# Block 4's scores alternate between two heads, a weight conversion runs two tiles ahead, and raw weights load in four pieces

## The chip, the cores and the metric

The kernel runs on one core of a Trainium2 chip. The metric is the device time of one execution in microseconds (us). Engines are named as in the profile: PE is TensorE's matmul, PEld its weight load, DVE is VectorE, ACT ScalarE, POOL GpSimd, SP SyncE. In this kernel every DMA is issued from SP, whose queue is in order: an issue that waits holds back all that stand behind it.

## The reference

Three layers follow each other. Attention works on q, k, v of shape (4, 8, 576, 64): causal softmax scores per head, with a second term from a stored memory `M_prev`, mixed by a gate.

```python
scores = scale * q @ k.T; masked above the diagonal; a = softmax(scores); local = a @ v
q_p = phi(q); mem_out = (q_p @ M_prev) / (q_p @ z_prev + 1e-6)
out = g * mem_out + (1 - g) * local
```

Its output, as x of 2304 tokens by 512, goes into MoE 1, a gated layer with d_ff = 1536: `x = (silu(x @ w_gate) * (x @ w_val)) @ w_out`. MoE 2 has 8 experts of width 1024 and a balanced router:

```python
P = exp(x @ w_gate - max)
for _ in range(8):                       # Sinkhorn
    P /= P.sum(1) + 1e-9; P /= P.sum(0) + 1e-9; P *= N / E
out = sum(P[:, e] * (relu(x @ w1[e]) @ w2[e]) for e in range(8))
```

## The kernel before

Matmuls are made from pairs of rounded parts: a value is split into a high part and the rest, and a product is three matmuls (high by high, high by low, low by high). `product` (L461) issues them for one output; `products` (L283) issues each of the three for all outputs of a list before the next one.

The source is not the order of the engines. The framework traces the program, and a list scheduler then orders each engine's instructions at compile time, by source order and by when its own cost model holds an instruction ready. An instruction that is ready by that model can so be put ahead of others written before it; on the chip each engine then runs its list in order. `issue_after(i)` binds each instruction of a block that is on the engine of `i` to stand behind `i`.

**Attention** (L147) handles 16 pairs of heads. Each has generators for its stages: `load`, `prepare`, `scores`, `normalize`, `transposed`, `values`. A written schedule, `BEGIN`, `ORDER` for the middle pairs and `END`, advances them one step at a time, several pairs interleaved; `S` is a step of `scores`. One pair's two heads lie on partitions 0 to 63 and 64 to 127, so a score matmul contracts over 64 rows. Query blocks are taken in the order 4, 3, 2, 1, 0. Blocks 3 to 1 (L344) compute both heads into one PSUM tile through `products`, which alternates the heads. Block 4 (L329) takes head 0 and then head 1, each a `ps` tile of its own, 576 keys as two halves of 288 columns; each head has 6 matmuls, one mask matmul (L336), a maximum on DVE (L338), an exponential on ACT (L339) and a `yield`. The pool `pss` has two buffers of two banks each. Block 0 (L364) is the last of a pair; its exponentials are L371.

**MoE 1** (L594) begins behind attention. Its weights arrive as 64-bit floats and are converted on the chip, 12 slices of the hidden width with 3 tiles each, 36 tiles. `load_unit` (L491) does a tile: a DMA of the raw words (`graw`, 3 buffers), then `narrow` (L469): ACT takes the magnitude (L481), POOL clips it (L482), DVE shifts (L483), restores the sign (L484), ACT rounds the high part (L485), DVE forms the low bits (L486 to L488); then a subtraction on DVE (L505) and a DMA that keeps the parts in DRAM for later passes (L506). `self.ahead` is the generator over all tiles. Two tiles are done at the end of attention, bound behind its last exponential, and `on()` (L610) advances `ahead` by one tile, or, when that is used up, the first generator of `aside`. The first pass computes token chunks 0 and 1 together, slice by slice, with `on(4)` ahead of it and three `on()` in each slice; the two matmul groups `hidden` end in a Silu on ACT (L618) and a product on DVE (L619). Later passes read the kept parts. Their `aside` work is, for a chunk that is done, the router's `logits` (L532: four copies and subtractions into `xl`, 2 buffers, eight matmuls, four transposes, in one step) and `parts` (L563: seven tiles of sums of x, split and written to DRAM by L561).

**MoE 2** (L976) takes 16 units of weights (half an expert each), and for each unit four chunks of 512 tokens (p = 0 to 3) and one of 256. `order` (L1021) is a string of steps: H is one group of 12 matmuls of `unit_hidden` (L884) on a tile `xr` of x, O one output group (`unit_out`, L956). `right` (L1002) loads `xr` through 5 buffers up to five tiles ahead. `prepare_unit` (L800) loads the next unit's raw weights as one DMA of 2 MB (L805; one buffer), then sums and splits them on POOL, ACT and DVE, one `yield` between the steps; it is advanced once a step from the first chunk's seventh step on. During unit 0 `aside` does the remaining logits and parts and the Sinkhorn iteration, at every second step of p = 0 and every step later.

## Time and profile before

| | |
|---|---|
| Time, median of three runs | 2288.07 us (2285.83 to 2288.82) |
| Profiled execution, time | 2287.38 us |
| Its span, first to last instruction | 2285.6 us |
| PE busy | 97% |
| DVE, ACT, POOL busy | 52%, 32%, 20% |
| Mean granted TensorE clock | 0.995 |

The span is what the instructions cover; the time has 1.8 us more around it. In the profile attention covers about the first 254 us, MoE 1 up to about 732 us, and MoE 2 the rest. Busy shares are means over stages with different limits: DVE is busy for 134.2 of the 152 us from 255 to 407 us and for about 45 of 96 us in a unit of MoE 2. A PE that is called busy can run at either clock.

### The profile page before, as it was taken

What the parts mean: (1) busy time and instruction counts of PE and PEld (TensorE: products, weight loads), DVE (VectorE), ACT (ScalarE), POOL (GpSimd) and SP (SyncE); (2) the same over time, 40 slices, a digit from 0 to 9 for tenths busy, and PEclk for the clock granted to TensorE, in tenths of its full rate; (3) what the DMA queues carried; (4) which work ended last, traced back from release to release, by engine and by line L of the source; (5) the groups of instructions that cost most, each with busy time, mean ns of one, the idle gap of its engine ahead of it and who ended that gap; (6) DMA issues with size and microseconds to landing.
All of it is one profiled execution on the core that took longest, in us unless ns stands there. A gap on an engine that the chain in (4) does not pass through costs nothing.

```text
span 2285.6 us, 33742 instructions
## 1 busy us (share of the span) xinstructions
PE 2224.9 (97%) x13490; PEld 1909.6 (84%) x13490; DVE 1191.8 (52%) x1915; ACT 737.1 (32%) x1452; POOL 466.2 (20%) x425
## 2 busy tenths in 40 slices
PE   8999898999999999999999999999999999999999
PEld 5666676778888788898888988888888898888998
DVE  7888788541413744544455444544445444454433
ACT  6887533331312322222222222222222222222221
POOL 6666555210201121101011010110101101011000
PEclk9999899999999999999999999999999999999999
DMA  4221477365532746546465464654646556465563
GB/s 167 102 102 66 139 236 233 123 233 212 190 135 100 283 132 223 196 145 227 143 230 194 147 221 147 227 192 154 221 145 221 192 162 212 142 227 195 164 200 133
DMA packets 112188, 406.45 MB, mean 178 GB/s; under 512 B 11680, under 2 KB 11680, under 8 KB 108960
## 3 DMA queue, kind: packets, MB, share of 16 engines
q1 hardware_dynamic: 112032, 404.29, 52.1%
q8 instruction: 108, 1.77, 0.3%
q14 instruction: 48, 0.39, 0.1%
HBM read 364.92 MB, written 39.32 MB: 177 GB/s over the span
## 4 chain that ended last, share of the span: by engine, by line
PE 82%; DMA 7%; DVE 5%; POOL 3%; issue 1%; ACT 1%; SPq 0%; ACTq 0%; DVEq 0%; POOLq 0%
PE po L465 37%; PE pt L884 13%; PE pc L884 10%; PE p L465 8%; DMA xr<-xp 6%; PE pt L947 4%; PE po L437 2%; PE pt L404 2%; POOL na L482 2%; PE ps L465 1%; PE ps L287 1%; POOL w L821 1%; DMA graw<-gvo 1%; PE pp L465 1%; ACT w L819 1%
## 5 line engine op out<-in xcount | busy, mean ns | idle before, releaser
L465 PE MATMUL po<-w,h 128*128 128x512 f32 x3456 | 835.2, 392 | 3.9 <-DVE nm L773 3.9
L465 PEld LDWEIGHTS po<-w,h 128*128 128x128 f32 x3456 | 631.5, 188 | 125.4 <-DVE nm L773 4.0
L884 PE MATMUL pt<-xr,w 128*128 128x256 f32 x3072 | 403.9, 280 | 0.0
L884 PEld LDWEIGHTS pt<-xr,w 128*128 128x128 f32 x3072 | 381.8, 188 | 6.8
L972 DVE SCALAR_TENSOR_TENSOR xacc<-po,Pw,xacc 128x512 f32<-128x512 f32 x270 | 202.3, 749 | 287.0 <-PE po L465 287.0
L465 PE MATMUL p<-xs,gw 128*128 128x512 f32 (+1 forms) x1440 | 312.8, 373 | 14.5 <-DVE hf L619 5.7
L884 PEld LDWEIGHTS pc<-xr,w 128*128 128x128 f32 x2304 | 296.5, 188 | 33.9 <-ACT w L819 19.3
L884 PE MATMUL pc<-xr,w 128*128 128x256 f32 x2304 | 305.8, 280 | 14.0 <-DMA xr<-xp 14.0
L465 PEld LDWEIGHTS p<-xs,gw 128*128 128x128 f32 x1440 | 253.3, 190 | 65.6 <-DVE hf L619 7.8
L891 ACT COPY m<-pc 128x512 f32<-128x512 f32 x192 | 112.2, 584 | 523.8 <-PE pc L884 523.8
L896 DVE TENSOR_TENSOR m<-pt,m 128x512 f32<-128x512 f32 x256 | 176.3, 690 | 191.2 <-PE pt L884 131.5
L903 ACT ACTIVATE h<-m 128x512 fp32r<-128x512 f32 x256 | 162.0, 633 | 285.9 <-DVE m L896 280.5
L904 DVE SCALAR_TENSOR_TENSOR h<-m,h 128x512 fp32r<-128x512 f32 x256 | 178.0, 696 | 79.1 <-ACT h L903 75.1
L815 POOL TENSOR_TENSOR w<-raw,w 128x512 fp32r<-128x512 f32 x17 | 22.5, 1322 | 745.9 <-ACT w L814 745.9
L465 PE MATMUL po<-h,ws 128*128 128x512 f32 x576 | 137.4, 390 | 0.0
L465 PEld LDWEIGHTS po<-h,ws 128*128 128x128 f32 x576 | 108.3, 188 | 22.8
L821 POOL TENSOR_TENSOR w<-raw,w 128x512 fp32r<-128x512 f32 x32 | 56.1, 1753 | 340.1 <-ACT w L819 340.1
L815 DVE TENSOR_TENSOR w<-ws,w 128x512 fp32r<-128x512 f32 x64 | 79.6, 1262 | 46.3 <-ACT w L814 44.2
L318 POOL TENSOR_SCALAR P<-P,sums 128x576 f32<-128x576 f32 (+4 forms) x160 | 94.6, 605 | 42.6 <-ACT ph L263 32.3
L482 POOL TENSOR_SCALAR na<-na 128x512 f32<-128x512 f32 x36 | 84.6, 2353 | 72.7 <-ACT na L481 56.9
L947 PEld LDWEIGHTS pt<-xr,w 128*128 128x128 f32 x768 | 94.3, 188 | 2.7
L619 DVE TENSOR_TENSOR sg<-sg,p 128x512 f32<-128x512 f32 (+1 forms) x48 | 29.6, 617 | 126.5 <-PE p L465 102.7
(180 smaller groups left out, 1989.4 us busy)
## 6 DMA issues: line engine op xcount, KB each, us to landing
xr<-xp SPq DMA_DIRECT2D x480, 512.0 KB, 4.1
raw<-w SPq DMA_DIRECT2D x16, 2048.0 KB, 8.1
gw<-kg SPq DMA_DIRECT2D x24, 1024.0 KB, 4.8
graw<-gvo SPq DMA_DIRECT2D x36, 512.0 KB, 4.2
xp<-xl SPq DMA_DIRECT2D x30, 512.0 KB, 3.3
kg<-gw SPq DMA_DIRECT2D x24, 512.0 KB, 3.8
ws<-ko SPq DMA_DIRECT2D x24, 512.0 KB, 4.7
qk<-qkv SPq DMA_DIRECT2D x16, 640.0 KB, 4.0
```

Source lines behind the costliest of these rows:

```text
L318: nc.gpsimd.tensor_scalar(t, t, r, 1.0, op0=ALU.mult, op1=ALU.mult)
L465: self.nc.tensor.matmul(out, lhs[a], rhs[b], start=start and n == 0, stop=stop and n == 2, skip_group_check=shared)
L482: nc.gpsimd.tensor_scalar(a, a, pattern(0x40000000), pattern(0x4FEFFE00), op0=ALU.max, op1=ALU.min)
L815: lo.tensor_sub(t[:, 1], q[name], f32(t[:, 0]))
L821: engine.tensor_sub(t[:, 1, j], raw[:, 2 * n + j, 1], f32(t[:, 0, j]))
L884: nc.tensor.matmul(out[:, j * HT:(j + 1) * HT], w[:, a, j, k], x[:, b, k], start=start and j + k + n == 0, stop=k + n == 3, skip_group_che ...
L891: nc.scalar.copy(t, src)
L896: nc.vector.tensor_add(c, *terms)
L903: nc.scalar.activation(t[:, 0], c, AF.Relu)
L904: nc.vector.scalar_tensor_tensor(t[:, 1], c, 0.0, f32(t[:, 0]), op0=ALU.max, op1=ALU.subtract)
L947: nc.tensor.matmul(ph[:, j * HT:(j + 1) * HT], w[:, b, j, k], x[:, c, k], start=j + a + k + i == 0, stop=a + k + i == 4, skip_group_check= ...
L972: nc.vector.scalar_tensor_tensor(acc, po, weight, acc, op0=ALU.mult, op1=ALU.add)
```

## The change

Attention: block 4 takes both `ps` tiles at once and issues its 12 matmuls with the heads alternating, then both masks; the maxima and exponentials follow one head a step, as before. MoE 1: the first two of a tile's operations after its DMA (magnitude on ACT, clip on POOL) move into `load_raw`, which is called two tiles ahead of the rest. The first three tiles' `load_raw` is called when the steps of `END` begin, outside the binding to the last exponential. Tiles are taken in an order that puts a slice's third tile one slice later. `on(4)` becomes `on(2)`, and `graw`, `na`, `nb` get 4, 4 and 3 buffers in place of 3, 3 and 4. `logits` yields after each split and before the transposes. MoE 2: the raw weights load as four DMAs of 512 KB, a step apart, and in the main loop these loads, like the DMAs of `aside`, are bound behind the latest `xr` load in SP's order; in unit 0 `aside` is advanced at every step.

```diff
@@ attention
-            for step, at in schedule(n):
+            steps = schedule(n)
+            for nth, (step, at) in enumerate(steps):
+                if nth == len(steps) - len(END.split()) and after:
+                    self.ahead = self.load_units()
+                    next(self.ahead)
@@ scores
-        for j, h in enumerate(HALVES):
-            ps = self.pss.tile([P, 2, 512], F32, name="ps")
-            for c in range(2):
-                self.product(
-                    ps[:, c, 0:hw], cut(q, h, slice(4 * P, 5 * P)), cut(k, h, slice(c * hw, (c + 1) * hw)), True, c != j
-                )
-            d = slice(0, P) if j == 0 else slice(hw - P, hw)
-            nc.tensor.matmul(ps[:, j, d], self.mask, self.identb, start=False, stop=True)
+        both = [self.pss.tile([P, 2, 512], F32, name="ps") for _ in HALVES]
+        for c in range(2):
+            for a, b in ((0, 0), (0, 1), (1, 0)):
+                for j, h in enumerate(HALVES):
+                    nc.tensor.matmul(
+                        both[j][:, c, 0:hw], q[a][h, 4 * P:5 * P], k[b][h, c * hw:(c + 1) * hw],
+                        start=a + b == 0, stop=a == 1 and c != j,
+                    )
+        for j, d in enumerate((slice(0, P), slice(hw - P, hw))):
+            nc.tensor.matmul(both[j][:, j, d], self.mask, self.identb, start=False, stop=True)
+        for j in range(2):
+            ps = both[j]
@@ narrow: magnitude and clip go to load_raw
-        nc.scalar.activation(a, high.bitcast(F32), AF.Abs, scale=65536.0)
-        nc.gpsimd.tensor_scalar(a, a, pattern(0x40000000), pattern(0x4FEFFE00), op0=ALU.max, op1=ALU.min)
@@ load_unit becomes load_raw and load_units
+    def load_raw(self, f, a):
+        raw = self.rawp.tile([P, 512, 2], I32, name="graw")
+        nc.sync.dma_start(raw, self.gvo[f, :, a].bitcast(I32).rearrange("p (n t) -> p n t", t=2))
+        t = self.nap.tile([P, 512], F32, name="na")
+        nc.scalar.activation(t, raw[:, :, 1].bitcast(F32), AF.Abs, scale=65536.0)
+        nc.gpsimd.tensor_scalar(t, t, pattern(0x40000000), pattern(0x4FEFFE00), op0=ALU.max, op1=ALU.min)
+        return raw, t
+    def load_units(self):
+        todo = sorted(((f, a) for f in range(NF1) for a in range(3)), key=lambda t: (t[0] + (t[1] == 2), t[1]))
+        begun = [self.load_raw(*t) for t in todo[:3]]
+        yield
+        for n, (f, a) in enumerate(todo):
+            if 0 < n < len(todo) - 2:
+                begun.append(self.load_raw(*todo[n + 2]))
...
+            w = self.narrow(*begun[n], parts[:, 0])
             nc.vector.tensor_sub(parts[:, 1], w, f32(parts[:, 0]))
             nc.sync.dma_start(kept, f32(parts))
             yield
@@ logits
             nc.vector.tensor_sub(t[:, 1], src, f32(t[:, 0]))
+            yield
...
         nc.vector.tensor_copy(lt[:, 0:m * P], pl[0:2 * E, 0:m * P])
+        yield
@@ moe1
-            on(4)
+            on(2)
@@ prepare_unit
-        nc.sync.dma_start(raw, self.w12[e, f:f + 4].rearrange("f p a n -> p f a n"))
-        yield
+        for n in range(4):
+            nc.sync.dma_start(raw[:, n], self.w12[e, f + n])
+            yield
@@ moe2
-                        nc.sync.dma_start(f32(tiles[-1]), self.xparts[q][k])
+                        self.last_load = nc.sync.dma_start(f32(tiles[-1]), self.xparts[q][k])
+            def behind(steps):
+                with tc.issue_after(self.last_load.ins):
+                    return next(steps, None)
-                        if u == 0 and (p or at % 2):
-                            next(aside, None)
+                        if u == 0:
+                            behind(aside)
-                            late = next(prep, None) == "late" or late
+                            late = behind(prep) == "late" or late
@@ body
-                for n, b in (("graw", 3), ("na", 3), ("nb", 4))
+                for n, b in (("graw", 4), ("na", 4), ("nb", 3))
```

## Rows read from the trace of the kernel before

**Rows 1.** The page, part 1: busy us, share of the span, instructions.
```profile
PE 2224.9 (97%) x13490; PEld 1909.6 (84%) x13490; DVE 1191.8 (52%) x1915; ACT 737.1 (32%) x1452; POOL 466.2 (20%) x425
```
**Rows 2.** PE's waits over the whole span: us in total, times, longest.
```profile
PE pc L884 <- DMA xr<-xp: 14.0, 15, 2.1
...
PE pt L404 <- DVE xacc L378: 5.9, 1, 5.9
PE p L465 <- DVE hf L619: 5.7, 5, 2.1
PE p L465 <- DVE sg L619: 4.8, 3, 2.1
PE p L542 <- DVE xl L540: 4.7, 5, 2.0
PE po L465 <- DVE nm L773: 3.9, 1, 3.9
PE p L465 <- DVE xs L457: 1.9, 1, 1.9
...
PE ps L287 <- ACT P L339: 1.6, 1, 1.6
...
PE po L542 <- DVE xl L540: 0.9, 1, 0.9
```
**Rows 3.** Three stretches: length, busy us (instructions) by engine, PEclk, DMA share, GB/s.
```profile
243.90:250.72 6.82, 5.63 (x23) 3.74 (x24) 4.84 (x12) 2.86 (x6) 0.95 (x1) 0.50 0.29 93
264.38:271.20 6.82, 5.80 (x14) 4.55 (x15) 5.01 (x10) 2.95 (x5) 4.60 (x2) 0.50 0.61 230
397.50:400.91 3.41, 3.41 (x10) 2.64 (x9) 3.22 (x7) 1.17 (x2) 2.03 (x1) 0.50 0.39 154
```
**Rows 4.** PE in order of time, one middle pair: start us, us, instruction.
```profile
107.38 0.40 PE L465 MATMUL ps<-KH,QH 64*128 64x288 f32 x1
...
108.37 0.23 PE L336 MATMUL ps<-identb,mask 128*128 128x128 bf16 x1
...
108.97 0.40 PE L465 MATMUL ps<-KH,QH 64*128 64x288 f32 x1
...
109.96 0.23 PE L336 MATMUL ps<-identb,mask 128*128 128x128 bf16 x1
...
111.50 0.47 PE L287 MATMUL ps<-KH,QH 64*128 64x448 f32 x2
...
112.31 0.29 PE L353 MATMUL ps<-identb,mask 128*128 128x128 bf16 x2
```
**Rows 5.** ACT in order of time, the same pair.
```profile
107.25 0.31 ACT L371 ACTIVATE P<-ps,nm 64x64 f32<-64x64 f32 x1
```
**Rows 6.** DVE in order of time, end of attention: idle before it and its releaser last.
```profile
241.06 1.48 DVE L483 TENSOR_SCALAR na<-na 128x512 int32<-128x512 int32 x1 [1.06 <-POOL na L482]
242.46 2.35 DVE L484 SCALAR_TENSOR_TENSOR na<-graw,na 128x512 int32<-128x512 int32 x2
244.73 0.21 DVE L378 COPY xacc<-pt 128x64 f32<-128x64 f32 x1
```
**Rows 7.** MoE 1's first pass, the stretch (columns as rows 3).
```profile
255.00:407.00 152.00, 138.29 (x578) 110.34 (x577) 134.22 (x236) 58.01 (x97) 79.83 (x34) 0.97 0.67 220
```
**Rows 8.** DVE by line, the same stretch: busy us, mean ns, idle before and releaser.
```profile
L483 DVE TENSOR_SCALAR na<-na 128x512 int32<-128x512 int32 x34 | 16.5, 489 | 14.6 <-POOL na L482 14.6
```
**Rows 9.** SP in order of time, unit 2 to 3 of MoE 2.
```profile
950.45 0.38 SPq L805 DMA_DIRECT2D raw<-w  x1
```
**Rows 10.** Landing of the five xr loads issued from 950.9 to 956.1 us.
```profile
DMA to landing us min/median/max: 9.8/9.9/10.4
```
**Rows 11.** The page, part 6: DMA issues, KB each, median us to landing.
```profile
xr<-xp SPq DMA_DIRECT2D x480, 512.0 KB, 4.1
raw<-w SPq DMA_DIRECT2D x16, 2048.0 KB, 8.1
```
**Rows 12.** ACT's waits from 239 to 407 us.
```profile
ACT na L481 <- DMA graw<-gvo: 49.2, 22, 4.0
```

More of the change, by code (lines that the diff above doesn't have):

```diff
@@ L467, in product, with narrow @@
             )
-    def narrow(self, raw, hi):
+    def narrow(self, raw, a, hi):
         nc = self.nc
-        n = raw.shape[1]
         low, high = raw[:, :, 0], raw[:, :, 1]
-        a = self.nap.tile([P, n], F32, name="na")
-        b = self.nbp.tile([P, n], F32, name="nb")
+        b = self.nbp.tile([P, 512], F32, name="nb")
         ai, bi = a.bitcast(I32), b.bitcast(I32)
-        nc.scalar.activation(a, high.bitcast(F32), AF.Abs, scale=65536.0)
-        nc.gpsimd.tensor_scalar(a, a, pattern(0x40000000), pattern(0x4FEFFE00), op0=ALU.max, op1=ALU.min)
         nc.vector.tensor_scalar(ai, ai, 4, 1, op0=ALU.logical_shift_left, op1=ALU.logical_shift_right)
@@ L489, in narrow @@
         return b
-    def load_unit(self, f):
+    def load_raw(self, f, a):
         nc = self.nc
-        for a in range(3):
-            raw = self.rawp.tile([P, 512, 2], I32, name="graw")
-            nc.sync.dma_start(raw, self.gvo[f, :, a].bitcast(I32).rearrange("p (n t) -> p n t", t=2))
+        raw = self.rawp.tile([P, 512, 2], I32, name="graw")
[5 more added lines that the diff above has]
+    def load_units(self):
+        nc = self.nc
+        todo = sorted(((f, a) for f in range(NF1) for a in range(3)), key=lambda t: (t[0] + (t[1] == 2), t[1]))
[4 more added lines that the diff above has]
+                begun.append(self.load_raw(*todo[n + 2]))
             if a == 0:
-                self.gw[f] = t = self.gwp.tile([P, 2, 2, 512], F32R, name="gw")
+                self.gw[f] = self.gwp.tile([P, 2, 2, 512], F32R, name="gw")
             if a < 2:
-                parts, kept = t[:, :, a], self.keptg[f][:, :, a]
+                parts, kept = self.gw[f][:, :, a], self.keptg[f][:, :, a]
             else:
-                self.ws[f] = t = self.wsp.tile([P, 2, 512], F32R, name="ws")
-                parts, kept = t, self.kepto[f]
-            w = self.narrow(raw, parts[:, 0])
+                self.ws[f] = self.wsp.tile([P, 2, 512], F32R, name="ws")
+                parts, kept = self.ws[f], self.kepto[f]
+            w = self.narrow(*begun[n], parts[:, 0])
             nc.vector.tensor_sub(parts[:, 1], w, f32(parts[:, 0]))
@@ L529, in open_early @@
         self.gw, self.ws = {}, {}
-        self.ahead = (step for f in range(NF1) for step in self.load_unit(f))
     def logits(self, psum, name, pool, first, last):
@@ L658, in more @@
                 if logits:
-                    self.logits(pgv, "p0", self.xl, t0 // P, (t0 + n) // P)
-                    yield
+                    yield from self.logits(pgv, "p0", self.xl, t0 // P, (t0 + n) // P)
                 yield from self.parts(c)
@@ L804, in prepare_unit @@
         e, f = u // 2, u % 2 * 4
-        nc.sync.dma_start(raw, self.w12[e, f:f + 4].rearrange("f p a n -> p f a n"))
-        yield
+        for n in range(4):
+            nc.sync.dma_start(raw[:, n], self.w12[e, f + n])
+            yield
         w1, w2 = self.w1[u], self.w2[u]
@@ L988, in start_up @@
                 for c in range(2, len(CHUNKS1)):
-                    self.logits(self.po, "po", xl, *(sum(CHUNKS1[c][0:k]) // P for k in (1, 2)))
-                    yield
+                    yield from self.logits(self.po, "po", xl, *(sum(CHUNKS1[c][0:k]) // P for k in (1, 2)))
                 yield from self.parts(PAIRS2 - 1)
```

## The prediction

> **What bounds the kernel now.** I read the page's busy shares first: PE works 2224.9 of 2285.6 us [rows 1], so no other engine bounds the whole, and a change pays only where PE waits, where it runs at the lower clock, or where its own work shrinks. Then the waits on PE [rows 2]: they are short and lie in four places, the end of attention (5.9), MoE 1's first pass (DVE's products L619, 5.7 and 4.8, and 1.9 for `xs`), the router's logits (4.7), and MoE 2 (3.9 once in unit 0, and 14.0 in 15 waits for `xr`). Third, the granted clock: three stretches behind such waits stand at 0.50, the 1.2 GHz level of the two (1.2 and 2.4 GHz) [rows 3]. Fourth, PE in order of time within a middle pair of attention, because the first part changes its own work [rows 4]. Last, who made DVE late: in MoE 1's first pass DVE is busy for 134.2 of 152 us [rows 7], and 14.6 of the rest it stands before L483 until POOL's clip is done [rows 8]. DVE is full there, and what it does in the wrong order PE pays for.
>
> **1. Block 4's scores.** One head's six matmuls of 288 columns run from 107.38 to its mask at 108.37, the other's from 108.97 to 109.96: 0.99 us each [rows 4]. Blocks 3 to 1, already alternating, show what two heads cost: six matmuls of 448 columns, both heads, take 0.81 us from 111.50 to the mask at 112.31, in rows of two that start together; 64 rows of one head and 64 of the other run side by side. Six pairs should so take what six singles take now, and one 0.99 goes per pair: 16 x 0.99 = 15.8. Against it: the second head now needs the second `ps` buffer at once and not 1.6 us later. That buffer holds the pair before's block 0, whose last exponential ends at 107.25 + 0.31 = 107.56 [rows 5], 0.18 after PE would start. With the way from ACT to PE I take 0.25 for 15 pairs: 3.8. That leaves 12.0. The top is 15.8; at the bottom each pair waits as long as PE's one wait for an exponential of this kind, 1.6 [rows 2], and 15.8 - 16 x 1.6 = -9.8. I take the value by the steady pair's own times, since that 1.6 is at the start. The Trainium skill, TensorEngine Tiling (Array Packing), section PSUM Bottleneck, says that packing speeds up the matmuls but not the emptying of PSUM; the 0.18 is that in this trace, and by the rule at its worst the gain would be the bottom just given.
>
> **2. End of attention.** The 5.9 us wait of L404 is for a DVE copy at 244.73 that empties a PSUM buffer. DVE is in order; before the copy stand L483 and L484 of the first two tiles, L483 waiting for POOL's clip (1.06 before the second) [rows 6]. The clips come late because magnitude and clip are bound behind the last exponential. In the change the first three are free of that bind, and their work is hidden where PE is the bound. DVE's operations may still stand ahead of the copy, 1.48 + 2.35 us for the last three of them, but can begin when DVE falls idle. Behind the wait PE did 5.63 us of work at half clock [rows 3], worth 2.8. So 8.7 at most; if 3.8 us of DVE work stays ahead, 5.9 - 3.8 = 2.1 and no clock, at least. I take 6.5, nearer the top.
>
> **3. Start of MoE 1.** `on(2)` puts four conversions, not six, ahead of the split of the second chunk; two conversions are up to 2 x 134.2 / 34 = 7.9 us of DVE (the 134.2 include products and splits [rows 7, 8]), more than the wait of 1.9 for `xs`. The half clock at 264.4 costs 5.80 / 2 = 2.9 [rows 3]. Together 4.8; I take 4.0, and 0 below. The missing fifth and sixth tiles aren't felt: slice 1 needs only tiles 0 to 3.
>
> **4. The rest of the first pass.** Waits for L619 of 10.5 (5.7 + 4.8), and 3.41 / 2 = 1.7 of clock: 12.2. With clips two tiles ahead DVE loses up to 14.6 of waiting, needs 137 for what took 152, and PE, busy 138.3 [rows 7], becomes the bound, barely. I take 9.0, because the two are so close that some products will still be late; 0 if POOL stays the slow one, 12.2 at the top. The added buffer of `graw` lets the DMA start one tile earlier and is what feeds this.
>
> **5. Logits in MoE 1.** The 4.7 us [rows 2] are PE standing between a split and its matmuls; now a step of matmul work lies between. I take 4.0, bounds 0 and 4.7. The twelve steps and the end of the generator make 13 `on()`, of which slice 0 has 13; the second chunk's leave one tile of `parts` behind the pass, some 1 us of ACT and DVE beside PE, cost 0 to 0.7.
>
> **6. Start of MoE 2.** The 0.9 for logits goes. The 3.9 stays: Sinkhorn's first copy L773 stands in DVE behind splits that wait for buffers of `xl`, and the writes that free these now queue in SP behind `xr` loads that wait for PE. I take 1.0; from -3.0 (the wait doubles, 0.9 - 3.9) to 4.8.
>
> **7. Raw weights.** The 2 MB load is issued at 950.45 [rows 9]. It takes 8.1 us to land, a load of 512 KB 4.1 [rows 11], and the five `xr` loads behind it take 9.8 to 10.4 [rows 10]: one queue, served in order. In the change a piece goes in behind the latest `xr` load, so the load that PE misses (issued at 950.93, held behind the 2 MB) passes ahead of all four; the next have one or two pieces before them, 2 us each (a quarter of 8.1), and are needed one to three steps later. I take 12.5 of the 14.0, bounds 0 and 14.0. Next late would be the unit's first sums on POOL, which wait for the last piece some 2 us longer, with the rest of the unit to catch up. Three more DMA issues a unit cost SP 3 x 0.38 [rows 9], beside PE.
>
> **Sum.** 12.0 + 6.5 + 4.0 + 9.0 + 4.0 + 1.0 + 12.5 = 49.0. The profiled execution took 2287.4 (span 2285.6 and 1.8 around it), 0.7 below the median: 2287.4 - 49.0 + 0.7 = 2239. All tops together, 15.8 + 8.7 + 4.8 + 12.2 + 4.7 + 4.8 + 14.0 = 65.0, give 2223.
>
> **Rivals.**
> - *MoE 1 stays bound by DVE* (parts 2 to 4 come out at a third, 6.5 for 19.5): 2239 + 13 = 2252. For it: DVE's 134.2 and PE's 138.3 are 4 us apart, and POOL's clips still run beside DVE. Against: the 14.6 us are waits, not work. 16%.
> - *PSUM eats the first part* (bottom of 1): 2239 + 21.8 = 2261. For it: two buffers, both taken at once. Against: the 0.18 above. 8%.
> - *Slower: ACT takes the magnitude of tile n+2 ahead of the rounding of tile n.* It stands so in the source; ACT then waits for the raw DMA with the rounding behind it, and DVE's last subtraction behind that. ACT's present wait for these DMAs is 49.2 us over 22, 2.2 each [rows 12]; 33 times 2.2 on DVE's path is 73, where the stretch has 152 - 134.2 = 18 spare: +55, and parts 2 to 4 gone: 2239 + 19.5 + 55 = 2313. It decides from a wait of (49.0 - 19.5 + 18) / 33 = 1.4 us a tile. For it: these waits exist. Against: ACT's list goes by readiness, and a fourth buffer gives the DMA a tile more of time. 6%.
> - *Slower: each piece pays a landing of its own*: 4 x 4.1 - 8.1 = 8.3 us later per unit, and the 15 units' waits grow by as much, +124: 2376. Against: the five `xr` loads behind the 2 MB were issued over 5.2 us and all landed within 10.4 [rows 10], so they don't add up. 2%. The Trainium skill, DMA: Bandwidth & Descriptors, section Bandwidth, asks for DMAs of at least 1 MiB, which speaks against the pieces; rows 10 speak against paying for it here.
> - *The lists come out as before*, since the scheduler decides: within 5 us of 2288. 3%.
>
> **How the numbers follow.** The forecast has 65%, with a range of its own of 2226 to 2252. The first two rivals (24%) are faster too. Slower is 8%, no change 3%, faster 89%; the run-to-run spread lets 0.2%, 4.6 us, be told from no change. The range is 2221 to 2268: it holds the forecast and the two near rivals, and leaves out the last three and some of their surroundings.
>
> **What would show it.** Part 1: block 4's matmuls as rows of two, a pair's period some 0.75 us shorter from one block 4 to the next, no wait for L371 over 0.3. Parts 2 to 4: no wait of L404 over 2.5 us, DVE's wait at L483 under 5 us in total, no stretch at 0.50 before 400 us. Part 5: waits at L542 under 1 us. Part 7: `xr` waits under 2 us in total, a unit some 0.9 us shorter. The forecast fails if DVE's first pass doesn't shorten, or if any new wait of PE exceeds 10 us in total.

## The result, and the profile after

The changed kernel takes 2267.13 us (2266.72 to 2267.34) beside 2288.45 for the kernel before: a ratio of 0.9909 [0.9889, 0.9928], faster by 21.3 us where 49 were forecast. The median is over four executions; one of them took 2649.98 us at a granted clock of 0.772, and the range and the ratio leave it out. The profiled execution took 2266.92 us, its span is 2264.8 and its granted clock 0.995, as before.

Three marks divide a span: the first matmul of block 4 in each of the 16 pairs, the first matmul of MoE 1 (`p<-xs,gw`) and the first of MoE 2 (`pc<-xr,w`). They are read from PE in order of time, and the same marks serve for every experiment below.

| us | before | after | difference | forecast |
|---|---|---|---|---|
| first matmul of MoE 1 (attention) | 254.2 | 264.3 | +10.1 | -18.5 (parts 1, 2) |
| from there to MoE 2 | 477.9 | 458.8 | -19.1 | -17.0 (parts 3 to 5) |
| from there to the end | 1553.6 | 1541.7 | -11.9 | -13.5 (parts 6, 7) |
| span | 2285.6 | 2264.8 | -20.8 | -49.0 |

So MoE 1 and MoE 2 gave about what was forecast, and the whole miss lies in attention, which became longer. Within it, block 4 of the sixth pair starts at 86.1 us (79.1 before), and from there the period of a pair is 14.86 (14.15 before). That is +7.0 in the first five pairs and +0.7 in each of the ten after them; the end of attention gives 3.8 back.

The busy shares of the page, part 1:

```profile
PE 2219.6 (98%) x13490; PEld 1904.9 (84%) x13490; DVE 1205.4 (53%) x1915; ACT 735.0 (32%) x1452; POOL 466.7 (21%) x425
```

PE's busy time fell by 5.3 us of 2224.9 [rows 1], for the same 13490 instructions. The rest of the gain is waiting. Waits on PE over the whole span (us in total, times, longest), which answer to [rows 2]:

```profile
...
PE pt L413 <- POOL P L322: 5.1, 12, 1.7
PE pt L904 <- DMA xr<-xp: 4.9, 1, 4.9
PE po L474 <- DVE xacc L988: 4.2, 1, 4.2
PE ps L291 <- ACT P L348: 4.1, 2, 3.5
PE pt L413 <- DVE xacc L387: 3.7, 1, 3.7
PE p L474 <- DVE sg L639: 3.6, 2, 2.8
PE ps L291 <- ACT P L368: 1.8, 10, 0.3
...
PE po L561 <- DVE xl L558: 1.0, 1, 1.0
PE p L474 <- DVE hf L639: 0.9, 1, 0.9
...
PE ps L338 <- ACT P L380: 0.3, 1, 0.3
```

The 15 waits of 14.0 for `xr` are gone, and so are those for `xl` in MoE 1 (the 1.0 that is left is in MoE 2); the products `sg` and `hf` keep PE 4.5 us where it was 10.5. New are the waits for POOL's P (L322), one of 4.9 for `xr` and one of 4.2 for `xacc`, both in unit 0. The wait for block 4's exponentials (L348, before L339) grew from 1.6 to 4.1, of which 3.5 stand in the first pair. The wait for the second `ps` buffer, L338 behind the exponential L380, is 0.3 once.

**A middle pair.** PE in order of time, the changed kernel (start, us, instruction):

```profile
115.76 0.40 PE L338 MATMUL ps<-KH,QH 64*128 64x288 f32 x1
...
116.11 0.40 PE L338 MATMUL ps<-KH,QH 64*128 64x288 f32 x1
...
117.10 0.28 PE L343 MATMUL ps<-identb,mask 128*128 128x128 bf16 x2
117.22 0.61 PE L403 MATMUL pt<-ident,ph 128*128 128x128 f32 x4
...
119.15 1.07 PE L446 MATMUL po<-T,vm 128*64 128x512 f32 x2
120.15 0.47 PE L291 MATMUL ps<-KH,QH 64*128 64x448 f32 x2
...
121.17 1.07 PE L446 MATMUL po<-T,vm 128*64 128x512 f32 x2
122.18 0.55 PE L413 MATMUL pt<-ident,P 128*128 128x128 f32 x3
```

The same view of the kernel before, places of the pair that [rows 4] did not reach:

```profile
108.44 0.60 PE L394 MATMUL pt<-ident,ph 128*128 128x128 f32 x4
...
110.12 0.87 PE L437 MATMUL po<-T,vm 128*64 128x384 f32 x4
...
112.53 1.08 PE L437 MATMUL po<-T,vm 128*64 128x512 f32 x4
113.53 0.66 PE L404 MATMUL pt<-ident,P 128*128 128x128 f32 x4
```

Block 4 with its masks takes 117.22 - 115.76 = 1.46 us. Before it was 1.06 for head 0 (107.38 [rows 4] to 108.44) and 1.15 for head 1 (108.97 to 110.12), so 0.75 is saved, as forecast. The price of the second buffer is in it: head 1's first matmul comes at 116.11, 0.35 after head 0's and 0.14 after ACT is done with the buffer (its last exponential of block 0, L380, runs from 115.66 to 115.97). Until then head 0's run alone, and head 1's last ones do so at the end. As PE is not idle meanwhile, no wait of that size shows. But the value products of 512 columns, which the change doesn't touch, come out otherwise. Before, four stand in a row, two of each head, and take 1.00 us from start to next start. After, head 0's two stand at 119.15 and head 1's two at 121.17, with block 3's scores between them, and each two take the 1.00 that four took. Each of these matmuls fills 64 of 128 columns (`128*64`): two heads' ran side by side where they were neighbours in the list, and not where block 3's scores stood between them. The Trainium skill, TensorEngine Tiling (Array Packing), section Key Properties, says that different tiles "can execute LdWeights and Matmul in parallel"; these rows agree, with 1.00 against 2.01, and add that the order of the list decides whether they do.

One whole pair as a stretch (length, busy us by engine, PEclk, DMA share, GB/s), first after, then before:

```profile
115.76:130.62 14.86, 14.50 (x99) 8.86 (x98) 13.97 (x27) 11.55 (x35) 9.29 (x15) 1.00 0.31 97
```
```profile
107.38:121.53 14.15, 14.15 (x100) 9.18 (x99) 11.71 (x27) 11.58 (x35) 9.79 (x14) 1.00 0.29 102
```

PE's work: 14.15 - 0.75 + 1.00 = 14.40, where the row has 14.50. The other 0.36 are two waits of 0.17 and 0.19 in this pair, L291 behind ACT's exponential L368 and L413 behind POOL's P. Together 14.86.

**The first pairs.** The first three tiles' magnitude and clip have only a DMA to wait for, so they stand at the start of attention and not at its end. What DVE does on these tiles stands there too. The bind behind the last exponential holds back what ACT does (the rounding, L489), but not DVE's shift, sign and low bits (L487, L488, L490 to L492), which need only the clip: fifteen operations, some 10 us, between 33.69 and 69.05 us. Clips and operations together are the early conversions below. POOL in order of time, the changed kernel:

```profile
31.74 5.68 POOL L503 TENSOR_SCALAR na<-na 128x512 f32<-128x512 f32 x3
37.91 2.42 POOL L322 TENSOR_SCALAR P<-P,sums 128x576 f32<-128x576 f32 x3 [0.49 <-DVE sums L299]
```

DVE and then PE in the same stretch:

```profile
35.58 0.82 DVE L487 TENSOR_SCALAR na<-na 128x512 int32<-128x512 int32 x1 [1.06 <-POOL na L503]
...
37.66 0.15 DVE L299 TENSOR_TENSOR sums<-sums,gs 128x4 f32<-128x4 f32 x1
```
```profile
38.81 0.66 PE L413 MATMUL pt<-ident,P 128*128 128x128 f32 x4 [1.71 <-POOL P L322]
```

Three clips hold POOL for 5.68 us. DVE, in order, stands 1.06 before a shift until the second clip is done, and the sums of the pair (L297 to L299) come between and behind its operations on the tiles. The P of the pair needs POOL and these sums: it waits 0.49 more for the sums when the clips are done, and PE waits 1.71 for P. Without these tiles (e3 below) the same P starts at 35.12 and not at 37.91. Two stretches, first after, then before:

```profile
25.20:40.80 15.60, 12.90 (x86) 7.31 (x85) 11.62 (x24) 13.02 (x39) 14.22 (x16) 1.00 0.25 88
40.80:56.60 15.80, 13.21 (x88) 8.46 (x86) 14.34 (x30) 9.18 (x26) 10.68 (x13) 0.89 0.45 130
47.60:51.02 3.42, 3.42 (x17) 2.08 (x17) 3.23 (x8) 2.29 (x8) 1.24 (x2) 0.50 0.79 245
```
```profile
24.00:36.00 12.00, 11.98 (x81) 7.65 (x80) 9.08 (x19) 10.88 (x37) 9.78 (x14) 1.00 0.26 90
36.00:50.70 14.70, 14.70 (x93) 9.02 (x92) 10.51 (x26) 10.76 (x30) 8.70 (x15) 1.00 0.29 99
```

Before, PE was full in the second and third pair. After, it is busy 12.90 of 15.60 and 13.21 of 15.80 us, and there is a stretch at half clock (47.60 to 51.02). In the third pair DVE is busy for 14.34 of 15.80 us, where it was 10.51 of 14.70.

**The end of attention.** DVE in order of time, the changed kernel, which answers to [rows 6]:

```profile
253.93 1.48 DVE L487 TENSOR_SCALAR na<-na 128x512 int32<-128x512 int32 x1 [2.73 <-POOL na L503]
...
256.05 0.22 DVE L387 COPY xacc<-pt 128x64 f32<-128x64 f32 x1
```

This is the fourth tile. Its magnitude is called two tiles ahead, and so still within the bind behind the last exponential; its shift stands in DVE ahead of the copy that PE waits 3.7 for, and waits 2.73 for its clip, as the first two tiles' did before.

**MoE 1's first pass.** The stretch that answers to [rows 7], and DVE's shift in it that answers to [rows 8]:

```profile
264.30:416.30 152.00, 146.29 (x633) 119.04 (x632) 132.25 (x226) 58.33 (x100) 79.39 (x33) 0.99 0.66 219
```
```profile
L487 DVE TENSOR_SCALAR na<-na 128x512 int32<-128x512 int32 x31 | 15.6, 508 | 7.9 <-POOL na L503 7.9
```

PE does 633 matmuls in 152 us where it did 578 and is busy for 146.29 (138.29 before); DVE's wait for the clip fell from 14.6 to 7.9.

**Unit 0 of MoE 2.** SP in order of time, and PE behind it:

```profile
757.11 0.60 SPq L825 DMA_DIRECT2D raw<-w  x1
758.49 0.32 SPq L581 DMA_DIRECT2D xp<-xl  x1
758.86 0.42 SPq L825 DMA_DIRECT2D raw<-w  x1
760.99 0.32 SPq L581 DMA_DIRECT2D xp<-xl  x1
761.40 0.44 SPq L1027 DMA_DIRECT2D xr<-xp  x1
```
```profile
767.85 2.90 PE L904 MATMUL pt<-xr,w 128*128 128x256 f32 x12 [4.89 <-DMA xr<-xp]
774.98 5.34 PE L474 MATMUL po<-w,h 128*128 128x512 f32 x16 [4.23 <-DVE xacc L988]
```

Here `xr` was issued at 761.40, behind writes of parts and two pieces of raw weights, and PE could start at 767.85.

### The profile page after: what moved, and what is told of

Its sections match the earlier page's. It is cut to its first block, busy times and chain, and to the rows that moved or that the text cites. A ratio compares the mean times of both kernels' runs of the same rounds, so it can differ in the third digit from the quotient of the medians.

```text
span 2264.8 us, 33872 instructions
## 1 busy us (share of the span) xinstructions
PE 2219.6 (98%) x13490; PEld 1904.9 (84%) x13490; DVE 1205.4 (53%) x1915; ACT 735.0 (32%) x1452; POOL 466.7 (21%) x425
## 4 chain that ended last, share of the span: by engine, by line
PE 80%; DVE 2%; DMA 2%; POOL 1%; issue 1%; ACT 0%; SPq 0%; POOLq 0%; ACTq 0%; DVEq 0%
PE po L474 39%; PE pt L904 15%; PE pc L904 11%; PE p L474 9%; PE pt L967 4%; DMA xp<-xl 1%; DMA raw<-w 1%; POOL na L503 1%; PE pp L474 1%; POOL ws L845 0%; DVE na L488 0%; DVE w L835 0%; DMA graw<-gvo 0%; DVE nb L491 0%; DVE nb L492 0%
## 5 line engine op out<-in xcount | busy, mean ns | idle before, releaser
L904 PE MATMUL pt<-xr,w 128*128 128x256 f32 x3072 | 403.8, 280 | 5.0 <-DMA xr<-xp 4.9
L904 PEld LDWEIGHTS pt<-xr,w 128*128 128x128 f32 x3072 | 381.7, 188 | 13.6 <-DVE w L841 5.1
L474 PE MATMUL p<-xs,gw 128*128 128x512 f32 (+1 forms) x1440 | 306.9, 370 | 6.5 <-DVE sg L639 3.6
L924 DVE SCALAR_TENSOR_TENSOR h<-m,h 128x512 fp32r<-128x512 f32 x256 | 191.8, 754 | 70.5 <-ACT h L923 65.8
L835 DVE TENSOR_TENSOR w<-ws,w 128x512 fp32r<-128x512 f32 x64 | 66.4, 1039 | 79.3 <-ACT w L834 77.0
L322 POOL TENSOR_SCALAR P<-P,sums 128x576 f32<-128x576 f32 (+4 forms) x160 | 92.3, 591 | 26.4 <-ACT Z L392 12.1
L967 PE MATMUL pt<-xr,w 128*128 128x256 f32 x768 | 95.3, 279 | 0.0
```

The lines of the kernel that those rows point to most:

```text
L322: nc.gpsimd.tensor_scalar(t, t, r, 1.0, op0=ALU.mult, op1=ALU.mult)
L474: self.nc.tensor.matmul(out, lhs[a], rhs[b], start=start and n == 0, stop=stop and n == 2, skip_group_check=shared)
L835: lo.tensor_sub(t[:, 1], q[name], f32(t[:, 0]))
L904: nc.tensor.matmul(out[:, j * HT:(j + 1) * HT], w[:, a, j, k], x[:, b, k], start=start and j + k + n == 0, stop=k + n == 3, skip_group_che ...
L924: nc.vector.scalar_tensor_tensor(t[:, 1], c, 0.0, f32(t[:, 0]), op0=ALU.max, op1=ALU.subtract)
L967: nc.tensor.matmul(ph[:, j * HT:(j + 1) * HT], w[:, b, j, k], x[:, c, k], start=j + a + k + i == 0, stop=a + k + i == 4, skip_group_check= ...
```

## The experiments

All in one table; the marks are of each one's profiled execution. "Sixth" is the start of the sixth pair's block 4, "period" the mean of the ten pairs after it, MoE 1 and MoE 2 the lengths between the marks. The ratio is to the kernel before on the same chip.

| run | time, us | ratio [interval] | sixth | period | start of MoE 1 | MoE 1 | MoE 2 |
|---|---|---|---|---|---|---|---|
| before | 2288.45 | 1 | 79.1 | 14.15 | 254.2 | 477.9 | 1553.6 |
| after | 2267.13 | 0.9909 [0.9889, 0.9928] | 86.1 | 14.86 | 264.3 | 458.8 | 1541.7 |
| e2 | 2297.02 | 1.0036 [1.0023, 1.0049] | 79.6 | 14.86 | 261.8 | 478.7 | 1555.1 |
| e1 | 2268.23 | 0.9912 [0.9897, 0.9927] | 91.8 | 14.15 | 263.2 | 459.4 | 1543.7 |
| e4 | 2256.96 | 0.9866 [0.9848, 0.9885] | 84.7 | 13.81 | 252.7 | 458.4 | 1542.2 |
| e12 | 2290.98 | 1.0003 [0.9992, 1.0015] | 80.2 | 13.80 | 251.3 | 478.0 | 1552.7 |
| e15 | 2293.86 | one run | 80.3 | 13.80 | 251.4 | 480.0 | 1560.7 |
| e3 | 2268.18 | 0.9909 [0.9895, 0.9924] | 80.1 | 14.86 | 260.3 | 461.9 | 1544.5 |
| e5 | 2254.49 | 0.9848 [0.9834, 0.9861] | 81.3 | 13.81 | 251.8 | 458.8 | 1545.2 |
| e13 | 2260.14 | 0.9865 [0.9843, 0.9887] | 79.1 | 14.16 | 255.3 | 457.1 | 1546.0 |
| e11 | 2263.96 | 0.9889 [0.9876, 0.9902] | 81.3 | 14.86 | 259.8 | 457.3 | 1543.8 |
| e9 | 2277.51 | 0.9950 [0.9938, 0.9963] | 80.1 | 14.85 | 261.1 | 473.5 | 1544.7 |
| e10 | 2274.01 | 0.9928 [0.9914, 0.9942] | 84.5 | 14.85 | 263.9 | 467.5 | 1542.1 |
| e7 | 2276.17 | 0.9942 [0.9928, 0.9955] | 84.6 | 14.87 | 264.0 | 457.9 | 1552.5 |
| e8 | 2265.38 | 0.9895 [0.9882, 0.9909] | 88.9 | 14.86 | 267.4 | 458.9 | 1539.8 |
| e6 | 2256.08 | 0.9847 [0.9834, 0.9861] | 80.3 | 13.81 | 250.5 | 458.3 | 1545.5 |
| e14 | 2253.78 | 0.9841 [0.9824, 0.9858] | 80.3 | 13.83 | 250.7 | 459.8 | 1541.3 |

### Block 4's scores (e2, e1, e4)

e2 is the kernel before with block 4's alternation alone; e1 is the changed kernel with block 4 as before:

```diff
-        for j, h in enumerate(HALVES):
-            ps = self.pss.tile([P, 2, 512], F32, name="ps")
...
+        both = [self.pss.tile([P, 2, 512], F32, name="ps") for _ in HALVES]
```

> The kernel before with block 4's new shape alone. Theory A: period 14.86, the value products split, the first pairs about 7 us late too, time 2288 + 13 = 2301. Rival B: the first pairs are not late, only the 0.7 a pair is lost: 2295. Rival C: the period shrinks by 0.74 as block 4's own matmuls do, time 2277.

> The changed kernel with block 4's scores as before (head 0, then head 1), all other edits kept. In the trace of the changed kernel a middle pair of attention takes 14.86 us instead of 14.15, and the 512-column value products of the two heads (one row of four starts in 1.0 us before) stand as two rows of 1.0 us with block 3's scores between them. Theory A (block 4's new shape makes the list scheduler split that row; the split costs 1.0 a pair): the period is 14.15 again, the row is whole, MoE 1 starts at about 250 us instead of 264.3, time 2253. Rival B (the three early clips on POOL, at 31.7 to 37.4 us, cost the first pairs some 7 us whatever block 4 does): period 14.15, but MoE 1 starts at about 257 and the time is 2260. Rival C (attention is slowed by something else of the change): 2267.

e2 is slower than before, by 0.0036 of 2288, 8.2 us, and it brings the period of 14.86, with the value products parted as in the changed kernel (two start at 112.65 and two at 114.68); its first pairs are not late, as its rival B had it. With e1 the period is 14.15 again. So the alternation alone makes the period longer, and no clip is needed for it. But e1 is not faster than the changed kernel, against its theory A: its sixth pair starts at 91.8, so a second loss, in the first pairs, belongs to another edit.

e4 is the changed kernel with the two heads' 512-column value products bound behind the latest mask of blocks 3 to 1, so that block 3's scores cannot come between them:

```diff
-                nc.tensor.matmul(ps[:, j, d], self.mask, self.identb, start=False, stop=True)
+                self.last_mask = nc.tensor.matmul(ps[:, j, d], self.mask, self.identb, start=False, stop=True)
...
-            for j, h in enumerate(HALVES):
-                v = s["v"][:, 2 * D * k + D * j:2 * D * k + D * j + D]
-                mm(po[h, k * P:], v, T[j][:, k, k * P:], start=False, stop=False)
+            with self.tc.issue_after(self.last_mask.ins) if k == 0 else ExitStack():
+                for j, h in enumerate(HALVES):
+                    v = s["v"][:, 2 * D * k + D * j:2 * D * k + D * j + D]
+                    mm(po[h, k * P:], v, T[j][:, k, k * P:], start=False, stop=False)
```

> The changed kernel with the 512-column value products bound behind the latest score mask in PE's list, which leaves the two heads' products together in all 16 pairs. Theory A: 1.0 us less in some 11 pairs, period about 13.85, time 2267 - 12 = 2255; with the two waits of 0.25 a pair gone as well 2250. Rival C (ACT's two exponentials in a row hold up the copies that the products wait for, so that the split only filled a wait): the row is whole but PE waits in front of it, period 14.6 to 14.9, time 2263 to 2267.

PE in order of time, and the pair as a stretch:

```profile
116.43 0.47 PE L291 MATMUL ps<-KH,QH 64*128 64x448 f32 x2 [0.24 <-ACT P L348]
...
117.46 1.08 PE L447 MATMUL po<-T,vm 128*64 128x512 f32 x4
118.47 0.32 PE L450 MATMUL pt<-F,vm 128*128 128x64 f32 x1
```
```profile
112.34:126.16 13.82, 13.58 (x99) 8.68 (x98) 12.17 (x27) 11.47 (x35) 10.27 (x15) 1.00 0.30 104
```

The four stand in a row again and take 1.01 us. The period is 13.81, 1.05 shorter than in the changed kernel, and MoE 1 starts 11.6 us sooner, ten times 1.05 and 1.1 more. Of the 0.75 saved, 0.24 now goes to a wait of block 3's scores for block 4's exponential (L348): PE reaches them sooner than ACT is ready. Another 0.18 is busy time, 13.58 where 14.15 - 0.75 is 13.40, in matmuls into `pt` that the edit doesn't touch; no run shows why. No term of the forecast had these two.

### The alternation once its side effect is undone (e12, e15, e13)

e12 is e2 with e4's binding; e15 is the same kernel in a second profile.

> The kernel before with block 4's alternating scores alone, and the 512-column value products of the two heads bound behind the latest score mask, so that they stand side by side. Theory (the alternation saves its 0.74 us a pair and pays 0.25 to 0.4 for the second PSUM buffer and the exponential; what made it slower was the split of the value products): the period of the steady pairs is 13.81 in place of 14.15, and the time is 2288 less 16 x 0.34 = 5.4, so 2282.6, between 2279 and 2286. Rival (the binding itself only helps together with the pipelined conversion): period 14.1 or more, time 2288 or above.

> The same kernel as e12 (block 4's alternation alone, value products kept together), a second profile. Theory (executions of one kernel differ in the first pairs of attention, by stretches at half clock there): a time of 2290 to 2292 comes with the sixth block 4 later by 6 to 10 us than e12's 80.16 and with the period 13.8 and MoE 1 and MoE 2 as long as there. Rival (they differ in MoE 2 or MoE 1): the sixth block 4 stands near 80 whatever the time.

The period came out as expected, 13.80, and attention is 2.9 us shorter than before. The time is not: 1.0003 [0.9992, 1.0015], an interval that leaves out a gain of 2.9 us (0.9987). So what attention gains is lost elsewhere. The two profiles show where executions of this kernel differ: attention agrees to 0.1 us, but MoE 1 differs by 2.0 and MoE 2 by 8.0, in code that the edit doesn't touch. My expectation that executions differ in the first pairs was wrong. Three stretches of the second profile that the first had at full clock:

```profile
865.13:868.54 3.41, 3.41 (x19) 3.41 (x18) 2.11 (x4) 1.49 (x3) 3.41 (x3) 0.50 0.83 311
1346.41:1349.82 3.41, 3.41 (x18) 3.41 (x17) 2.11 (x3) 1.80 (x4) 3.41 (x3) 0.50 0.85 318
1732.12:1735.53 3.41, 3.41 (x18) 3.41 (x18) 2.11 (x3) 1.67 (x3) 3.41 (x3) 0.50 0.61 202
```

They follow the waits for `xr` of units 1, 6 and 10 (1.91, 1.82 and 2.77), and the waits are 16.0 in total where the first profile has 13.6; a stretch at half clock in unit 0 is 6.83 long in place of 3.41. Four times 1.7 us of clock and 2.4 of waiting are 9.2 at most, for the 8.0 that MoE 2 differs by. The length of a wait alone does not decide: one of 1.87, at unit 1 of the first profile, had no such stretch behind it. The mean granted clock is 0.993 over e12's twelve executions and 0.994 over the seventeen of the kernel before beside them; why it is lower is left open. The changed kernel doesn't have these waits.

e13 is e5 (below) without alternation and binding:

```diff
-        both = [self.pss.tile([P, 2, 512], F32, name="ps") for _ in HALVES]
...
+        for j, h in enumerate(HALVES):
+            ps = self.pss.tile([P, 2, 512], F32, name="ps")
```

> The changed kernel with block 4's scores one head after the other as before, and the first three tiles' magnitudes bound behind the latest exponential at the start of the end of attention. Beside e5 (the same with alternating scores and value products kept together, 2254.5) it lacks the alternation alone. Theory (the alternation is worth its period, 14.15 - 13.81 = 0.34 a pair over some 15 pairs): 2254.5 + 5 = 2259.5, between 2257 and 2263, period 14.15. Rival (the alternation gives its gain back in the first pairs and at the end, so it is worth nothing): within 2 us of 2254.5.

MoE 1 starts at 255.3 in place of 251.8 in e5, and the ratios stand at 0.9865 and 0.9848, with intervals that overlap. By the marks the alternation with its pairs kept is worth 3 to 3.5 us of attention (e12 and here), a quarter of the 12 forecast; that the whole time gains by it is not shown. Not all of its 0.35 a pair arrives: the sixth pair starts 1.1 to 2.2 us later than without it.

### The early clips (e3, e5, e11)

e3 binds the first three tiles behind attention's last exponential, as the first two were; e5 is e4 with their magnitudes bound behind the latest exponential at the start of `END`:

```diff
                 if nth == len(steps) - len(END.split()) and after:
                     self.ahead = self.load_units()
-                    next(self.ahead)
+                    with tc.issue_after(self.last_exp.ins):
+                        next(self.ahead)
```

> The changed kernel with the first three tiles' load, magnitude and clip bound behind the last exponential of attention, as before. Theory A: the early pairs stay as late as in the changed kernel (MoE 1's start moves only by what the end of attention gains or loses, 0 to 4 us): 2267 to 2271. Rival B: the early pairs are some 5 us earlier: 2262.

> The kernel with the value products kept together (the run before, 2257) and, beside it, the first three tiles' magnitudes bound behind the latest exponential at the point where the steps of END begin, so that they run near 220 us instead of 30 us. The run with the clips behind the very last exponential had its sixth pair's block 4 at 80.1 us, the changed kernel at 86.1. Theory D (POOL's three clips at 31 to 37 us stand in front of the scaling that PE's transposes wait for, and cost the early pairs 5 to 6 us, clock included): sixth pair about 79, time 2251. Rival (the early pairs' loss is block 4's own): sixth pair 84 to 85, time 2257.

In e3 the first pairs are as fast as in e2: the sixth starts 6.0 us sooner than in the changed kernel. The end of attention is 2.0 longer, so that MoE 1 starts 4.0 sooner, and MoE 1 is 3.1 longer: PE waits 4.4 for `xacc` and 3.6 for `xs`. The time is the same. So the early conversions moved a cost from the end of attention to its start, and the time shows no gain by them. e3 and e5 both move POOL's clips and DVE's operations on the tiles together; how the cost parts between the two, no run shows. e5 has neither cost in full: sixth pair 81.3, MoE 1 458.8, but waits of 1.8 and 1.8 at the end. It is faster than e4 by 0.0018, which the intervals don't tell apart.

e11 is e4 with the three tiles placed in the middle of attention:

```diff
+                if after and step == "S" and at in (7, 8, 9) and (steps[nth - 1] != (step, at)) and at not in begun:
+                    begun.append(at)
+                    if at == 7:
+                        self.ahead = self.load_units()
+                    with tc.issue_after(self.last_exp.ins):
+                        next(self.ahead)
```

> The changed kernel with the 512-column value products of the two heads kept together (bound behind the latest score mask) and with the first three tiles' DMA, magnitude and clip placed one each in the pairs whose scores begin as numbers 7, 8 and 9, behind the latest exponential. Theory: the early pairs lose nothing to the clips (sixth block 4 at 79 to 82), the period stays 13.81 in pairs without a clip and grows by less than 1 us in those with one, the end of attention waits less than with the clips at its own start (3.6 us there): MoE 1 starts near 249, time about 2250, between 2247 and 2254. Rival (a clip of about 2 us on POOL delays the masked products P of its pair wherever it stands): each of the three pairs is 1.5 to 2 us longer, MoE 1 starts near 254, time about 2256.

The rival was right in that each tile costs where it stands, and too mild. The steps from pair to pair are 15.5, 17.8, 17.9 and 14.6 there and 13.8 elsewhere: 10.6 us for three tiles, with waits of up to 1.26 behind DVE and stretches at half clock. But PE does not wait for P there, as the rival had it: 4.8 of the 5.2 it waits in these pairs are behind DVE (T and `pz`), and DVE itself stands 1.00, 3.13 and 2.73 before the three shifts until POOL's clip is done. A pair of attention had no room for a tile's clip and what DVE does with it.

In all sixteen kernels the sixth mark goes by this placement: 79.1 to 81.3 without an early conversion and 84.5 to 91.8 with three, whatever else differs.

### MoE 1 (e9, e10)

e9 has the conversion as before (the diff of `narrow`, `load_unit`, `on(4)` and the buffers, taken back); e10 has `logits` in one step:

```diff
             nc.vector.tensor_sub(t[:, 1], src, f32(t[:, 0]))
-            yield
...
         nc.vector.tensor_copy(lt[:, 0:m * P], pl[0:2 * E, 0:m * P])
-        yield
```

> The changed kernel with the conversion of MoE 1's weights as it was (magnitude and clip within each tile, no early tiles, tiles in slice order, on(4), buffers 3, 3, 4); block 4, logits and MoE 2 stay changed. Theory (parts 3 and 4 are the pipelining's): DVE stands some 14 us before its shift again, PE's waits for DVE's products sg and hf come back to about 10 us, and MoE 1 goes from 458.8 to 470 to 474 us. With no early clip on POOL the first pairs of attention come about 6 us sooner (sixth block 4 near 79.6), and the wait at the end of attention returns (3.7 to about 5.9): 2267 + 13 - 6 + 2 = 2276, between 2270 and 2284. Rival (MoE 1 gained by its logits and by its later start against DVE's backlog, the pipelining adds nothing): MoE 1 stays below 462 us, waits for sg and hf under 6 us, time about 2263.

> The changed kernel with the router's logits in one step again. Theory (part 5): PE's waits for the split xl, 1.0 us now, come back to about 5.6 us (4.7 in MoE 1, 0.9 in MoE 2), and the time is 2267 + 4.5 = 2271.5. Rival (the wait for xl only stands in for another late operand of the same pass): waits for xl return but the time stays within 2 us of 2267.

e9: DVE by line and the stretch that answers to [rows 7, 8], then PE's waits in it.

```profile
L489 DVE TENSOR_SCALAR na<-na 128x512 int32<-128x512 int32 x34 | 17.6, 520 | 19.2 <-POOL na L488 19.2
```
```profile
262.00:414.00 152.00, 135.74 (x569) 107.75 (x568) 130.15 (x230) 57.24 (x97) 80.86 (x34) 0.98 0.67 218
```
```profile
PE p L471 <- DVE hf L627: 7.8, 5, 2.1
PE p L471 <- DVE sg L627: 5.2, 4, 2.1
```

All of it came back: the wait for the clip, the waits of PE, 569 matmuls in 152 us, and MoE 1 14.7 us longer. So the conversion's edit shortened the pass; its parts (clips ahead, the order of the tiles, `on(2)`, the buffers) were not run apart. e10: the waits for `xl` are back too (4.7 and 1.9), with a stretch at half clock from 444.83 to 448.24; MoE 1 is 8.7 us longer and the ratio 0.0019 higher, 4.3 us, with intervals that overlap. Forecast was 4.0.

### MoE 2 (e7, e8, e6, e14)

e7 loads raw weights in one DMA and keeps the order behind `xr`; e8 keeps the pieces and drops the order; e6 is e5 with unit 0's raw loads one chunk later; e14 is e5 with e8's edit:

```diff
# e7
-        for n in range(4):
-            nc.sync.dma_start(raw[:, n], self.w12[e, f + n])
-            yield
+        nc.sync.dma_start(raw, self.w12[e, f:f + 4].rearrange("f p a n -> p f a n"))
+        yield
# e8, e14
-                            behind(aside)
+                            next(aside, None)
...
-                            late = behind(prep) == "late" or late
+                            late = next(prep, None) == "late" or late
# e6
-                        if p == (u == 0) and at == 6:
+                        if p == 2 * (u == 0) and at == 6:
...
```

> The changed kernel with the raw weights as one DMA of 2 MB again, still bound behind the latest xr load. If the four pieces took away the 13.8 us of xr waits of units 1 to 15, those come back: 2267 + 12 = 2279. If the place in SP's order did it (the xr load that PE missed now passes ahead), the waits stay away: 2267 to 2270.

> The changed kernel with four pieces, but neither these nor unit 0's side work bound behind the xr loads. If the pieces alone take away the xr waits: under 3 us of them in units 1 to 15, 2262 to 2267 (unit 0's waits may change). If the binding did it: 6 to 13 us of waits come back, 2273 to 2280.

> The run e5 with one more edit: in unit 0 the raw weights of unit 1 load from p = 2 on and not from p = 1. The changed kernel has two new waits there, 4.9 us for xr at 763 and 4.2 for po at 771, and 10 us at half clock. Theory E (the raw pieces and the writes of xp share SP's queue with the xr loads in p = 1, and a piece or a write that waits holds them back): both waits shrink under 2 us, 6 to 9 us less than e5. Rival (the writes of xp alone do it, since they wait for DVE with xr loads behind them): the same waits, the same time as e5 within 2 us.

> e5 (2254.5) with the raw loads and the DMAs of aside no longer bound behind the latest xr load. Theory (the new waits of unit 0 come from that order: e8, without it, had 5.0 us of xr waits there and none for xacc, against 9.1 to 9.5): unit 0 gains about 4 us, MoE 2 takes 1541 or less from its first matmul, time 2250.5, between 2248 and 2253. Rival (the wait moves to the Sinkhorn copies, as in e6): the waits of unit 0 keep their sum of some 9.5, time within 2 us of 2254.5.

PE's waits for `xr`, e7 and then e8:

```profile
PE pt L903 <- DMA xr<-xp: 16.6, 5, 9.6
```
```profile
PE pt L904 <- DMA xr<-xp: 4.5, 1, 4.5
PE pc L904 <- DMA xr<-xp: 0.5, 1, 0.5
```

Either edit alone removes the waits of units 1 to 15: 1.7 is left there in e7 and nothing in e8. The forecast had given the gain to both together. What the pieces bring besides is unit 0, where e7 waits 14.9. The new waits of unit 0 did not go by a change of order: in e6 they became 3.8 behind Sinkhorn's copies, 2.4 for `xr` and 2.1 for `xacc`; in e14 5.3 for `xacc`, 1.9 for ACT's `m` and 1.6 for `xr`. Why unit 0 has so little slack is left open.

e14 is the fastest kernel run, 2253.78 us at 0.9841 [0.9824, 0.9858], but not to be told from e5 or e6. e5's interval [0.9834, 0.9861] lies below that of the changed kernel.

## Why the prediction was wrong

| part | forecast | measured | from |
|---|---|---|---|
| 1 Block 4's scores | -12.0 | +7.6 | start of MoE 1, e2 against before |
| 2 end of attention | -6.5 | +2.5 | the rest of attention's +10.1 (against e2: end -3.9, sixth pair +6.5) |
| 3, 4 first pass | -13.0 | -14.7 | MoE 1, e9 against after |
| 5 logits | -4.0 | -4.4 | the rest of MoE 1's -19.1 |
| 6 start of MoE 2 | -1.0 | +2.3 | units 0 and 1 of MoE 2 |
| 7 raw weights | -12.5 | -14.2 | units 2 to 15 |

Part 1 failed, as the step "one 0.99 goes per pair: 16 x 0.99". Its own arithmetic held in the steady pairs, where block 4 saves 0.75, and that by some luck: head 1 came 0.35 late and not 0.25 (0.21 to the end of the exponential and 0.14 from ACT to PE, for which the prediction took 0.18 and, from no row, 0.07), and the two masks, now together, gave 0.11 back. Wrong was to take the rest of the pair's list as given. The prediction's rivals looked for new waits; the price came as busy time of PE, the same matmuls in another order, 1.00 us a pair (14.15 to 14.50 busy, and e4 takes it back). Its sign that a new wait above 10 us would overturn it could not see this; its sign of a period 0.75 shorter does, with 0.71 longer. Its bound for the first part, a loss of 9.8, was near the outcome, for another reason: it thought of a stall for PSUM in every pair, and PE's wait for that is 0.3 once.

Part 2 failed as well, at "their work is hidden where PE is the bound". PE was the bound, but POOL's clips and DVE's operations on the same tiles stood ahead of the sums and of P, on which PE's transposes wait a moment later: +6.5 us by the sixth pair. The cover was there for PE and not for POOL and DVE. The end itself gave 3.9. Its wait fell by only 2.2, to 3.7, near the 2.1 that was named as the least gain, because the prediction counted three tiles, and the fourth, still bound behind the last exponential, now stands where the first two stood. What the early conversions save at the end (2.0 of attention and 3.1 of MoE 1 by e3) they cost at the start (6.0).

Parts 3 and 4 were right in size, and in cause by e9. Part 5 was right in kind by e10; its size lies between 4.3 by the ratio and 8.7 by the marks. DVE's own wait went to 7.9 and not below 5, without harm, since PE is busy for 146.29 of the 152 us. The clock did not come back as forecast: before there were 20.5 us at half clock in four stretches ([rows 3] and one of 3.41 in unit 0), after six of 3.41, also 20.5, two of them in the first pairs.

Part 7 was right: no wait for `xr` in units 1 to 15, and a unit is 14.2 / 14 = 1.0 us shorter (0.9 forecast). Its reason was half right, since either of its two edits does it. Part 6 came out near its bad bound, a loss of 3.0, by the two new waits of unit 0, and its own two terms the other way round: the 3.9 behind Sinkhorn's copy is gone, and the wait for logits stays, 1.0. The `xr` load that PE waits for stands on SP behind writes and pieces, where part 6 had writes behind `xr` in mind; as other orders (e6, e14) only moved the waits, that this order is the cause is not shown.

Of the rivals none is what happened. "PSUM eats the first part" gave 2261, by a wait that isn't there; "MoE 1 stays bound by DVE" is excluded by the 19.1 us that MoE 1 gave, and ACT's waits for the raw words fell from 49.2 [rows 12] to 23.3 (249 to 417 us). That the time lies inside the range of 2221 to 2268 is luck: its slow end was there for the PSUM rival.

## What to carry to other kernels

Where a list scheduler orders the instructions, an edit that makes one group shorter is priced on the whole period: look for matmuls that run side by side only as neighbours, compare their order in both lists, and bind them together if they part. Before work is moved to an earlier stage because PE is full there, read each engine that it runs on in that stage, and what PE waits for from that engine next; a bind on one engine's instructions holds back only those, and not what other engines do with the same tile. Test two edits that aim at one wait separately; here one was enough.

## What the runs showed of the hardware that was not expected

Executions of one kernel can differ by the clock behind short waits: three stretches of 3.41 us at 0.50 stand behind `xr` waits of 1.82 to 2.77 us in one execution of a kernel (e15) and not in another (e12), whose time was 10.2 us less, and there a wait of 1.87 had none behind it. In these two attention repeats to 0.1 us. It does not where three tiles are converted early in it: the changed kernel, e7 and e10 have the same lists of attention on every engine, and their sixth pair starts at 86.1, 84.6 and 84.5 us, 4 to 7 us later than without these tiles.
